# Attention and feed-forward on one core: unsplit float32 products on halves of the array, transposes on VectorE and by SBUF transfers

## The chip, the cores and the metric

The kernel runs on one core of a Trainium2 chip. The time is device time in microseconds (us) of one execution; the number compared is the median of several runs. Five engines work side by side: TensorE (PE, with its weight loads as PEld), VectorE (DVE), ScalarE (ACT), GpSimd (POOL) and SyncE (SP), which here issues all transfers. Matrix products go from SBUF to PSUM; SBUF and PSUM have 128 partitions.

## What is computed

Attention with a threshold, then a feed-forward layer. Inputs are q, k, v of shape (8, 8, 576, 64), a scalar tau, w_in (512, 2048), w_out (2048, 512) and scalars s and b; the output is (4608, 512), all float32.

```python
scores = scale * np.matmul(q, k.transpose(0, 1, 3, 2))       # scale = 1/8
thresh = np.max(scores, axis=-1, keepdims=True) - tau
scores = np.where(scores >= thresh, scores, -1000000000.0)
scores = scores - np.max(scores, axis=-1, keepdims=True)
attn = np.exp(scores)
attn = attn / (np.sum(attn, axis=-1, keepdims=True) + 1e-09)
x = np.matmul(attn, v)              # then (batch, seq, heads * 64)
h = x @ w_in
g = s * np.maximum(h, 0.0) ** 2 + b
out = g @ w_out
```

## The kernel before

Queries are worked on in tiles of 128 rows. A sequence has 576 rows: four full tiles and a tail of 64, and the tails of two heads share one tile. A visit is a batch, a pair of heads and a half of the sequence: four full tiles, and in half of the visits a tail tile. 64 visits make 288 tiles.

For each tile (`tile_of`), scores of 128 queries by 576 keys go to a PSUM bank (L329); VectorE scales and copies them to `sm` with the row's minimum of the negated scores (L332); ScalarE takes exp into `em` (L338); VectorE zeroes what is under the threshold and sums (L341); GpSimd normalizes (L349). TensorE transposes `em` in four blocks of 128 and one of 64 (L358 `tp`, L359 `tt`), because the product with v needs keys on the partitions. The result, 64 columns for each head, goes to `x`.

A float32 number is used in one of two ways. For the first batch (class `Plain`, the first 36 tiles) the products are plain float32, one head at a time: scores with 64 rows of the array, values (L374) with 64 columns. For the others (class `Head`) each operand is split in a high and a low part of type fp32r. The two parts of q lie on the two halves of the rows, those of v on the two halves of the columns, and k and the transposed attention are split in two tensors each; so scores take two products for each half of the keys (L329), and values nine products (L405). The splits cost copies on ScalarE (L279, L287, L292, L389, L391) and subtractions on VectorE (L288, L392, L394, L412) and GpSimd (L280, L293); k, q and part of v are loaded twice, once for each half of the partitions (L250, L258, L263).

The feed-forward layer takes blocks of 256 rows of x: 18 blocks (16 full ones and 2 of tails), with 16 steps for each (`Block.step`). A step makes 12 products of 256 columns into bank `h` (L536), ReLU, square and the high part on ScalarE (L539, L541, L542), the low part on GpSimd (L543), and six products of 512 columns into bank `o` (L549). `Block.stage` splits a block of x (L519, L521). The weights come as float32 and are split once, in 16 groups, on ScalarE and VectorE (`weights`, L466 to L477), into an accurate high and low part.

The order on every engine is written by class `Plan`: each operation is added with an engine, a cost, the keys it reads and writes, and a due time in tiles (`at`). `Plan.run` goes through time with these costs and takes, on each free engine, the ready operation that is due first. Constants set the due times: `LOAD_AHEAD`, `SCORES_AHEAD`, `VALUES_AFTER` and `FFN_AFTER` in tiles, `WEIGHTS_AT` and `WEIGHTS_EACH` for the conversion of weight group f (at `WEIGHTS_AT + WEIGHTS_EACH * f`). `keep_busy` (L677) adds products without use at the start.

Of the kernel before, what the change touches and what calls it, by code (L numbers as in the profile page):

```python
# [22 lines left out]
TWO_BANKS = 16  # L26
WEIGHTS_AT, WEIGHTS_EACH = 12, 1.5
# [80 lines left out]
def tile_attention_ffn(ctx: ExitStack, tc: tile.TileContext, qT, kT, v, tau, w_in, w_out, s, b, out):  # L108


# [14 lines left out]
    HS = S // 2  # L125

# [19 lines left out]
    st = [const(f"st{i}", [P, 8]) for i in range(6)]
    smem = [tuple(const(f"{n}{i}", [P, S + 1]) for n in ("sm", "em")) for i in range(2)]
    qs = [const(f"q{j}", [P, NB], F32R) for j in range(2)]
    raw_head = const("rk", [P, S]), const("rq", [P, S]), const("rv", [P, 5, D])
    xb = [const(f"x{i}", [P, NC, NB]) for i in range(3)]  # L150
    xt = const("xt", [P, NC, 4 * T])
    oo = const("oo", [P, 2, DM])
# [3 lines left out]
        ("s", [P, 2, 512]), ("o", [P, 2, DM]), ("tp", [P, NQ, P]), ("tt", [P, 512]), ("pv", [P, 512]), ("h", [P, 512]))}  # L156
# [4 lines left out]
    def claim(keys, fn):  # L161

        old = [k for k in list(plan.writer) + list(plan.readers) if isinstance(k, tuple) and k[0] == keys[0]]
        plan.add("-", (0, 0), fn, [], list(dict.fromkeys(old)) + keys, -100)


    def split_buffers():
        def e():
            t = sb("e", [P, 9, 3 * P], F32R)
            lazy["ehi"], lazy["elo"] = t[:, 0:5], t[:, 5:9]  # L170

        def k():
            lazy["k"] = sb("k", [P, 4, S], F32R)

        def v_():
            lazy["v"] = sb("v", [P, 3, 5, 2, D], F32R)
        claim(["e"] + [(n, c) for n in ("eh", "el", "et") for c in range(6)], e)
        claim(["k", "khi0", "klo0", "khi1", "klo1"], k)
        claim(["v", "v0", "v1", "v2"], v_)
        claim(["e32", "oo0", "oo1"] + [("x", 2, c, j, u) for c in range(NC) for j in range(2) for u in range(2)], lambda: None)  # L180

    def pe(n, cols, fn, r, w, at):

        plan.add("PE", (n * (0.44 * cols + 6.5), n * (0.44 * cols + 6.5) + 170), fn, r, w, at)
# [4 lines left out]
    def dve2(cost, fn, r, w, at):  # L189
        plan.add("DVE", cost, fn, r, w, at, True)  # L190
# [7 lines left out]
    def dma(kb, fn, r, w, at):  # L198
        plan.add("SP", (max(550, kb * 3.6), 2200 + kb * 3.6), fn, r, w, at)


    class Plain:


        def __init__(self, bi, p_):
            self.bi, self.p, self.tag = bi, p_, ("w%d" % (NF - 1), "v", "k", "e")[p_]
            self.keys = [(self.tag, n) for n in ("k", "q", "v0", "v1")]

        def get(self):
            if self not in lazy:  # L210
                t = sb(self.tag, [P, 2 * S - T + 10 * D], F32)
                lazy[self] = t[:, 0:S], t[:, S:2 * S - T], t[:, 2 * S - T:].rearrange("p (h t d) -> p h t d", h=2, t=5)
            return lazy[self]

        def load(self, at):
            kk, kq = self.keys[:2]
            h2 = slice(2 * self.p, 2 * self.p + 2)
            dma(295, lambda: nc.sync.dma_start(out=self.get()[0], in_=kT[self.bi, h2].rearrange("h d s -> (h d) s")),
                [], [kk], at)
            dma(262, lambda: nc.sync.dma_start(out=self.get()[1], in_=qT[self.bi, h2, :, 0:M].rearrange("h d s -> (h d) s")),  # L220
                [], [kq], at)
            for j in range(2):
                h = 2 * self.p + j
                dma(128, lambda j=j, h=h: nc.sync.dma_start(
                    out=self.get()[2][:, j, 0:NQ], in_=v[self.bi, h, 0:M, :].rearrange("(p t) d -> p t d", t=NQ)),
                    [], [self.keys[2 + j]], at)
                dma(16, lambda j=j, h=h: nc.sync.dma_start(out=self.get()[2][0:T, j, NQ], in_=v[self.bi, h, M:S, :]),
                    [self.keys[2 + j]], [self.keys[2 + j] + (1,)], at)

        def load_tail(self, at):  # L230
            for j in range(2):
                dma(16, lambda j=j: nc.sync.dma_start(
                    out=qd[self.p % 2][j * D:(j + 1) * D, j * T:(j + 1) * T], in_=qT[self.bi, 2 * self.p + j, :, M:S]),
                    [f"qd{self.p % 2}"], [(f"qd{self.p % 2}", j)], at)

    class Head:
        def __init__(self, i, bi, h, q0, q1, tail):
            self.i, self.bi, self.h, self.j, self.q0, self.q1, self.tail = i, bi, h, h % 2, q0, q1, tail

        def load(self, at):  # L240

            q0, q1 = self.q0, self.q1
            rk, rq, rv = raw_head
            self.parts = [], [], []

            def put(which, name, buf, cols, ap, kb):
                for o in 0, D:
                    keys = [(name, o, c) for c in range(cols.start // T, cols.stop // T)]
                    self.parts[which].extend(keys)
                    dma(kb, lambda o=o: nc.sync.dma_start(out=buf[o:o + D, cols], in_=ap), [], keys, at)  # L250

            put(0, "rk", rk, slice(0, S), kT[self.bi, self.h], 144)
            q1_ = S if self.tail and q1 == M else q1
            put(1, "rq", rq, slice(q0, q1_), qT[self.bi, self.h, :, q0:q1_], 64)
            if self.tail and q1_ < S:
                put(1, "rq", rq, slice(M, S), qT[self.bi, self.h, :, M:S], 16)
            self.parts[2].append(("rv", 0))
            dma(128, lambda: nc.sync.dma_start(out=rv[:, 0:NQ, :],  # L258
                                               in_=v[self.bi, self.h, 0:M, :].rearrange("(p t) d -> p t d", t=NQ)),
                [], [("rv", 0)], at)  # L260
            for o in 0, D:
                self.parts[2].append(("rv", 1 + o))
                dma(16, lambda o=o: nc.sync.dma_start(out=rv[o:o + D, NQ, :], in_=v[self.bi, self.h, M:S, :]),  # L263
                    [], [("rv", 1 + o)], at)

        def prepare(self, at):
            pk, pq, pv_ = self.parts
            j = self.j
            rk, rq, rv = raw_head
            q0, m = self.q0, self.q1  # L270
            self.kks, self.kqs, self.kts = [f"khi{j}", f"klo{j}"], [f"q{j}"], [f"qt{j}"]

            def khi():
                return lazy["k"][:, 2 * j]

            def klo():
                return lazy["k"][:, 2 * j + 1]
            self.q, self.ks = (lambda: qs[j]), (lambda: [khi(), klo()])
            act((580, 675), lambda: nc.scalar.copy(out=khi(), in_=rk), pk, [f"khi{j}"], at)  # L279
            pool((1420, 1450), lambda: nc.gpsimd.tensor_tensor(out=klo(), in0=rk, in1=khi().bitcast(F32), op=ALU.subtract),  # L280
                 pk + [f"khi{j}"], [f"klo{j}"], at)

            parts = [(slice(q0, m), qs[j], f"q{j}", (305, 405), (400, 430))]
            if self.tail:
                parts.append((slice(M, S), qt[:, j, j * T:(j + 1) * T], f"qt{j}", (150, 245), (190, 220)))
            for cs, dst, key, ca, cd in parts:
                act(ca, lambda dst=dst, cs=cs: nc.scalar.copy(out=dst, in_=rq[:, cs]), pq, [key], at)  # L287
                dve2(cd, lambda dst=dst, cs=cs: nc.vector.tensor_tensor(  # L288
                    out=dst[D:P], in0=rq[D:P, cs], in1=dst[D:P].bitcast(F32), op=ALU.subtract), pq + [key], [key], at)
            i = self.i % 3  # L290
            self.kvs, self.v = [f"v{i}"], lambda: lazy["v"][:, i]
            act((360, 460), lambda: nc.scalar.copy(out=self.v()[:, :, j, :], in_=rv), pv_, self.kvs, at)  # L292
            pool((850, 885), lambda: nc.gpsimd.tensor_tensor(out=self.v()[:, :, 1 - j, :], in0=rv,  # L293
                                                             in1=self.v()[:, :, j, :].bitcast(F32), op=ALU.subtract),
                 pv_ + self.kvs, self.kvs, at)


    class Group:


        def __init__(self, hd, c0, n, dests):
            self.hd, self.c0, self.n, self.dests, self.blocks = hd, c0, n, dests, []
# [484 lines left out]
```

## Time and profile before

| | |
|---|---|
| runs | 1405.14, 1397.42, 1398.55 us; median 1398.55 |
| profiled execution, first to last instruction | 1402.1 us |
| TensorE busy | 1384.8 us (99%) |
| VectorE busy | 1066.8 us (76%) |
| ScalarE busy | 986.8 us (70%) |
| GpSimd busy | 736.3 us (53%) |
| granted TensorE clock | 1.00 throughout |
| from HBM, to HBM | 88.21 MB, 9.44 MB |

The page gives the profiled execution's span and no time of its own; the span is 3.6 us, or 0.25%, above the median of the runs. Busy time of TensorE is modelled from pipelined records, so the pitch from one start to the next says more than a duration. In a row of the timeline the first number is the start in us from the span's start, the second the length, and xN how many records of one kind are merged; `128*64 128x256` is the part of the array (rows * columns) and the operand's shape. A row of a group shows count, busy us, mean ns of one, and idle time ahead of it with what ended it.

### The profile page before, as it was taken

Reading aid. Unit: us, or ns where it says so; the run is one execution under the profiler, and the core shown is the slowest. Engines: PE = TensorE matmul, PEld = TensorE weight load, DVE = VectorE, ACT = ScalarE, POOL = GpSimd, SP = SyncE. Lnnn points to the kernel's source line nnn. Section 1 sums busy time; section 2 is a strip of 40 time slices with the busy share of each in tenths; the row PEclk is TensorE's granted clock in tenths of the full one; section 3 lists DMA queues with packets and bytes.
Section 4 is the critical chain, followed back from the end, with each engine's and each line's share of the span. In section 5 each row is a group of like instructions: output and inputs, shape, how many; then the busy total and the mean of one; then the engine's idle time right before and its main releaser. Section 6 shows DMA issues by size and latency. Waiting matters only on the chain.

```text
span 1402.1 us, 29393 instructions
## 1 busy us (share of the span) xinstructions
PE 1384.8 (99%) x9369; PEld 1252.3 (89%) x9369; DVE 1066.8 (76%) x3099; ACT 986.8 (70%) x2487; POOL 736.3 (53%) x798
## 2 busy tenths in 40 slices
PE   9999999999999999999999999999999999999998
PEld 7678789889899989998999999999999999999887
DVE  4977568988998898878888787888788887887101
ACT  3777557867777777777777777777777777776443
POOL 1233336656676656655566555665566555564210
PEclk9999999999999999999999999999999999999999
DMA  9701112221222222222122122222222222220000
GB/s 301 248 26 35 29 39 66 82 74 55 79 74 87 63 76 70 81 60 70 52 84 72 55 73 64 83 60 66 65 71 71 70 66 72 64 75 15 16 16 16
DMA packets 94539, 99.59 MB, mean 71 GB/s; under 512 B 34480, under 2 KB 72368, under 8 KB 94384
## 3 DMA queue, kind: packets, MB, share of 16 engines
q1 hardware_dynamic: 94384, 97.71, 23.5%
q8 instruction: 74, 1.21, 0.4%
q14 instruction: 81, 0.66, 0.1%
HBM read 88.21 MB, written 9.44 MB: 70 GB/s over the span
## 4 chain that ended last, share of the span: by engine, by line
PE 93%; DVE 3%; ACT 2%; issue 1%; POOL 0%; DMA 0%; DVEq 0%; SPq 0%; ACTq 0%; POOLq 0%
PE h L536 28%; PE o L549 28%; PE s L329 12%; PE pv L405 9%; PE tp L358 9%; PE pv L374 3%; PE tt L359 2%; DVE em L341 1%; PE h L677 1%; PE h L488 1%; PE o L329 1%; DVE sm L332 1%; DVE e L392 0%; ACT em L338 0%; ACT g L539 0%
## 5 line engine op out<-in xcount | busy, mean ns | idle before, releaser
L536 PE MATMUL h<-xh,w 128*128 128x256 f32 x2304 | 465.5, 285 | 5.0 <-ACT g L539 4.8
L349 POOL TENSOR_SCALAR em<-em,st 128x576 f32<-128x576 f32 x288 | 251.9, 875 | 273.3 <-DVE st L346 113.2
L536 PEld LDWEIGHTS h<-xh,w 128*128 128x128 f32 x2304 | 376.4, 190 | 15.8 <-ACT g L539 8.9
L549 PE MATMUL o<-w,gh 128*128 128x512 f32 x1152 | 369.6, 402 | 0.6 <-ACT g L539 0.5
L543 POOL TENSOR_TENSOR gl<-g,gh 128x256 fp32r<-128x256 f32 x272 | 217.4, 799 | 263.8 <-ACT gh L542 93.6
L536 PE MATMUL h<-xl,w 128*128 128x256 f32 x1152 | 325.4, 282 | 0.2
L341 DVE SCALAR_TENSOR_TENSOR em<-sm,st,em 128x577 f32<-128x577 f32 x288 | 255.3, 887 | 34.5 <-ACT em L338 25.8
L332 DVE TENSOR_SCALAR_CACHE_REDUCE sm<-s 128x576 f32<-128x576 f32 x280 | 211.2, 754 | 89.2 <-PE s L329 86.9
L338 ACT ACTIVATE em<-sm,st 128x576 f32<-128x576 f32 x288 | 224.9, 781 | 49.2 <-DVE sm L332 44.6
L539 ACT ACTIVATE g<-h 128x256 f32<-128x256 f32 x288 | 109.1, 379 | 187.6 <-PE h L536 184.2
L549 PE MATMUL o<-w,gl 128*128 128x512 f32 x576 | 225.9, 392 | 0.1
L536 PEld LDWEIGHTS h<-xl,w 128*128 128x128 f32 x1152 | 219.1, 190 | 5.7 <-DVE xl L521 0.6
L549 PEld LDWEIGHTS o<-w,gh 128*128 128x128 f32 x1152 | 196.4, 189 | 25.9 <-ACT g L539 0.8
L392 DVE TENSOR_TENSOR e<-tp,e 128x512 fp32r<-128x512 f32 (+1 forms) x280 | 178.0, 636 | 53.7 <-ACT e L389 50.0
L389 ACT CAST e<-tp 128x512 fp32r<-128x512 f32 (+1 forms) x280 | 150.5, 538 | 64.3 <-PE tp L358 59.9
L280 POOL TENSOR_TENSOR k<-rk,k 128x576 fp32r<-128x576 f32 x112 | 169.7, 1515 | 45.3 <-ACT k L279 41.9
L358 PE MATMUL tp<-ident,em 128*128 128x128 f32 x1152 | 175.2, 275 | 1.9 <-POOL em L349 0.8
L329 PE MATMUL s<-k,q 128*128 128x288 f32 x896 | 165.4, 306 | 0.3 <-DVE sm L332 0.3
L358 PEld LDWEIGHTS tp<-ident,em 128*128 128x128 f32 x1152 | 137.1, 140 | 26.3 <-issue 5.4
L405 PE MATMUL pv<-e,v 128*128 128x320 f32 (+1 forms) x1008 | 152.6, 296 | 0.0
L405 PEld LDWEIGHTS pv<-e,v 128*128 128x128 f32 x1008 | 141.4, 189 | 2.3
L329 PEld LDWEIGHTS s<-k,q 128*128 128x128 f32 x896 | 130.1, 189 | 4.4 <-DVE sm L332 0.9
(108 smaller groups left out, 1799.3 us busy)
## 6 DMA issues: line engine op xcount, KB each, us to landing
rk<-in_k_dram SPq DMA_DIRECT2D x224, 144.0 KB, 2.8
rv<-in_v_dram SPq DMA_DIRECT2D x112, 128.0 KB, 2.1
rq<-in_q_dram SPq DMA_DIRECT2D x168, 64.0 KB, 2.3
w<-in_moe_w_in_dram SPq DMA_DIRECT2D x16, 512.0 KB, 8.6
w<-in_moe_w_out_dram SPq DMA_DIRECT2D x16, 512.0 KB, 8.7
out_dram<-oo SPq DMA_DIRECT2D x32, 256.0 KB, 2.2
rq<-in_q_dram SPq DMA_DIRECT2D x56, 80.0 KB, 2.4
rv<-in_v_dram SPq DMA_DIRECT2D x224, 16.0 KB, 2.0
```

What stands on the lines that cost most here:

```text
L280: pool((1420, 1450), lambda: nc.gpsimd.tensor_tensor(out=klo(), in0=rk, in1=khi().bitcast(F32), op=ALU.subtract), pk + [f"khi{j}"], [f"klo ...
L329: nc.tensor.matmul(ps[:, hf, 0:HS], stat, kk[:, cs], start=(n == 0), stop=(n == len(seq) - 1))
L332: dve((760, 840), lambda: nc.vector.tensor_scalar(out=get()[0][:, 0:S].rearrange("p (a b) -> p a b", a=2), in0=ps[:, :, 0:HS], scalar1=-SC ...
L338: act((690, 785), lambda: nc.scalar.activation(out=get()[1][:, 0:S], in_=get()[0][:, 0:S], func=AF.Exp, bias=st8[:, 0:1], scale=-1.0), [sm ...
L341: dve2((830, 930), lambda: nc.vector.scalar_tensor_tensor(out=get()[1], in0=get()[0], scalar=st8[:, 1:2], in1=get()[1], op0=ALU.is_le, op1 ...
L349: pool((800, 835), lambda: nc.gpsimd.tensor_scalar(out=get()[1][:, 0:S], in0=get()[1][:, 0:S], scalar1=st8[:, 4:5], scalar2=st8[:, 5:6], o ...
L358: nc.tensor.transpose(out=tp[:, t, :], in_=em[:, t * P:(t + 1) * P], identity=ident)
L392: dve((60 + 560 * big, 140 + 560 * big), lambda hi=hi, lo=lo, cs=cs: nc.vector.tensor_tensor(out=lo(), in0=tp[:, :, cs], in1=hi()[:, 0:NQ] ...
L405: nc.tensor.matmul(ps, g.hd.v()[:, kt, :, :], o[:, kt], start=(n == 0), stop=(n == len(seq) - 1))
L536: nc.tensor.matmul(ps, w[:, c, :], x[:, c, :], start=(i == 0), stop=(i == 3 * NC - 1))
L543: do((715, 750), lambda: eng.tensor_tensor(out=lo, in0=g, in1=hi.bitcast(F32), op=ALU.subtract), [f"g{k}", f"gh{k}"], [f"gl{k}"], at)
L549: nc.tensor.matmul(bank["o"][:, t, :], a[:, ts_], w, start=(f == 0 and i == 0), stop=(f == NF - 1 and i == 2))
```

## The change

No tile is split any more; `Plain`, `Head` and `Group` give way to one class `Visit`. The first batch is treated like the others.

- Scores (`scores`): k and q of a pair of heads are loaded once, one head on partitions 0 to 63 and the other on 64 to 127. One group of four float32 products makes the scores of a tile of both heads, each head on its half of the array's rows, into its own bank (`s0`, `s1`). A tail tile takes two products with all rows.
- Values (`with_v`): one group of ten float32 products for each visit, each head on its half of the array's columns, into one bank.
- Transposes: VectorE transposes blocks of 32 by 32 within `em` into `tr` (two instructions a tile), and four transfers a tile from `tr` to `er`, issued by SyncE, put the blocks where the values' product reads them. The order of keys in v's load follows that.
- Of the small operations, the threshold's addition goes to ScalarE (`AF.Identity`), and the case of an empty row is left to a sum that can't vanish, with the threshold's sign handled once.
- Due times: `VALUES_AFTER` 2 instead of 1, `FFN_AFTER` 2.5 instead of 1.5, weights at 6 + 1.2 f instead of 12 + 1.5 f. `Plan` gets new costs, and VectorE's operations are no longer kept apart from GpSimd's in it. `oo` is one buffer instead of two.

```diff
-LOAD_AHEAD, PREPARE_AHEAD = 6, 2.5
-SCORES_AHEAD, VALUES_AFTER = 1, 1
-FFN_AFTER = 1.5
+LOAD_AHEAD = 6
+SCORES_AHEAD, VALUES_AFTER = 1, 2
+FFN_AFTER = 2.5
-WEIGHTS_AT, WEIGHTS_EACH = 12, 1.5
+WEIGHTS_AT, WEIGHTS_EACH = 6, 1.2
...
+    class Visit:
+        def load(self, at):
+            n, bi, h2 = self.n, self.bi, self.h2
+            dma(295, lambda: nc.sync.dma_start(out=kb[n], in_=kT[bi, h2].rearrange("h d s -> (h d) s")), [], [("k", n)], at)
...
+            for j in range(2):
+                dma(131, lambda j=j: nc.sync.dma_start(
+                    out=vb[n][:, j, 0:NQ], in_=v[bi, 2 * self.pair + j, 0:M, :].rearrange("(c p) d -> p c d", p=P)),
+                    [], [self.kv[j]], at + 1)
...
+    def scores(vs, i, t):
...
+        def pairs():
+            for hf in range(2):
+                cs = slice(hf * HS, (hf + 1) * HS)
+                for j in range(2):
+                    r = slice(j * D, (j + 1) * D)
+                    nc.tensor.matmul(bank[f"s{j}"][:, hf, 0:HS], qb[n][r, t * P:(t + 1) * P], kb[n][r, cs],
+                                     start=True, stop=True)
...
+        def blocks():
+            nc.vector.transpose(out=to[:, :, 0:NQ].rearrange("p m c q -> p m (c q)"),
+                                in_=ev[:, 0:M].rearrange("p (m r) -> p m r", m=4))
+            nc.vector.transpose(out=to[:, 0:2, NQ], in_=ev[:, M:S].rearrange("p (m q) -> p m q", m=2))
+        dve((915, 980), blocks, [em_k], [tr_k], i + 0.5)
+        for n in range(4):
+            jj, e = (n // 2, NB // 32 + n % 2) if t is None else (j, 4 * t + n)
+            plan.add("SP", (450, 2600), lambda n=n, jj=jj, e=e: nc.sync.dma_start(
+                out=er[:, vs.n, jj, e], in_=to[32 * n:32 * n + 32].rearrange("p m c q -> p m (c q)")),
+                [tr_k], [("er", vs.n, jj, e)], i + 0.5)
+
+    def with_v(vs, at):
...
+            for c in range(5):
+                for j in range(2):
+                    nc.tensor.matmul(ps[j * D:(j + 1) * D, 0:32 * nb], vb[n][:, j, c], er[:, n, j, 0:nb, 32 * c:32 * c + 32],
+                                     start=(c == 0), stop=(c == 4))
```

More of the change, by code (lines that the diff above doesn't have):

```diff
@@ L7 @@
 from concourse._compat import with_exitstack
-from concourse.masks import make_identity
 F32 = mybir.dt.float32
@@ L155, in tile_attention_ffn, with pe @@
     bank = {n: pp.tile(sh, F32, name=n) for n, sh in (
-        ("s", [P, 2, 512]), ("o", [P, 2, DM]), ("tp", [P, NQ, P]), ("tt", [P, 512]), ("pv", [P, 512]), ("h", [P, 512]))}
+        ("s0", [P, 2, 512]), ("s1", [P, 2, 512]), ("o", [P, 2, DM]), ("pv", [P, 512]), ("h", [P, 512]))}
     lazy = {}
     plan = Plan()
[L161 to L184, printed above, removed]
+    def pe(cost, fn, r, w, at):
+        plan.add("PE", (cost, cost + 170), fn, r, w, at)
     def dve(cost, fn, r, w, at, port=False):
@@ L189, in dve2 @@
     def dve2(cost, fn, r, w, at):
-        plan.add("DVE", cost, fn, r, w, at, True)
+        plan.add("DVE", cost, fn, r, w, at)
     def act(cost, fn, r, w, at):
@@ L236, in tile_attention_ffn @@
[L236 to L295, printed above, removed]
@@ L328, in scores @@
-                for n, (stat, kk) in enumerate(seq):
-                    nc.tensor.matmul(ps[:, hf, 0:HS], stat, kk[:, cs], start=(n == 0), stop=(n == len(seq) - 1))
-        pe(2 if plain else 4 * len(ti.heads), HS * (3.7 if plain else 1), scores, ti.kq(), [bk], i - SCORES_AHEAD)
-        dve((760, 840), lambda: nc.vector.tensor_scalar(
-            out=get()[0][:, 0:S].rearrange("p (a b) -> p a b", a=2), in0=ps[:, :, 0:HS], scalar1=-SC,
-            scalar2=None, op0=ALU.mult, op1=ALU.min, accum_out=st8[:, 0:1]), [bk], [sm_k, (ks_, 0)], i - SCORES_AHEAD)
@@ L349, in tile_of @@
-        pool((800, 835), lambda: nc.gpsimd.tensor_scalar(
-            out=get()[1][:, 0:S], in0=get()[1][:, 0:S], scalar1=st8[:, 4:5], scalar2=st8[:, 5:6], op0=ALU.mult,
-            op1=ALU.add), [em_k, (ks_, 4), (ks_, 5)], [em_k], i)
-        tp, tt = bank["tp"], bank["tt"][0:T, 0:P]
-        def transposes():
-            em = get()[1]
-            for t in range(NQ):
-                nc.tensor.transpose(out=tp[:, t, :], in_=em[:, t * P:(t + 1) * P], identity=ident)
-            nc.tensor.transpose(out=tt, in_=em[:, M:S], identity=ident)
@@ L654, in tile_attention_ffn @@
-    pairs = [Plain(0, p_) for p_ in range(NP)]
-    heads = [Head(2 * vi + j, vis[0], 2 * vis[1] + j, vis[2] * P, vis[3] * P, vis[4])
-             for vi, vis in enumerate(visits) for j in range(2)]
-    tiles, first = [], {}
-    for vi, vis in enumerate(visits):
-        for ti in make_tiles(vis, *((pairs[vis[1]],) * 2 if vis[0] == 0 else heads[2 * vi:2 * vi + 2])):
-            for hd in ti.heads:
-                first.setdefault(hd, len(tiles))
-            tiles.append(ti)
-    n_plain = sum(ti.plain is not None for ti in tiles)
@@ L666, in tile_attention_ffn, with constants @@
-    pairs[0].load(-30)
+            xs[bi, u] = len(xs) % 3
+            for p_ in range(NP):
+                visits.append(Visit(len(visits), bi, p_, u, (bi > 0 and p_ < NP // 2) == (u == 0)))
+    tiles = []
+    for vs in visits:
+        vs.first = len(tiles)
+        tiles += [(vs, j, t) for t in range(2) for j in range(2)]
+        if vs.tail:
+            tiles.append((vs, 0, None))
+        vs.last = len(tiles) - 1
+    def constants():
+        for t in range(2):
+            nc.gpsimd.memset(sm[t][:, S:S + 1], -3e38)
+            nc.gpsimd.memset(em[t][:, S:S + 1], 1e-9)
+            nc.gpsimd.memset(tr[t][:, 2:4, NQ], 0.0)
+            nc.gpsimd.memset(vb[t][:, :, NQ], 0.0)
+            nc.gpsimd.memset(qd[t], 0.0)
+        nc.gpsimd.memset(zero, 0.0)
@@ L667, in tile_attention_ffn @@
+    pool((900, 900), constants, [], ["sm0", "sm1", "em0", "em1", "tr0", "tr1"] +
+         [("v", n, 2 + m) for n in range(2) for m in range(2)] + [("qd", n, j) for n in range(2) for j in range(2)], -9)
+    visits[0].load(-30)
     dma(0.5, lambda: nc.sync.dma_start(out=tau_t, in_=tau.partition_broadcast(P)), [], ["tau"], -20)
@@ L692, in tile_attention_ffn @@
     events = []
-    for p_, pr in enumerate(pairs):
-        if p_:
-            events.append((0, lambda pr=pr: pr.load(first[pr] - LOAD_AHEAD)))
-        t = n_plain - 5 * (NP - p_) + 2
-        events.append((0 if p_ < 2 else t - 9, lambda pr=pr, t=t: pr.load_tail(t - 6)))
-    events.append((n_plain - 0.2, split_buffers))
-    for hd in heads:
-        if hd in first:
-            events.append((n_plain - 0.1 if first[hd] < n_plain + 1 else first[hd] - 0.5,
-                           lambda hd=hd: (hd.load(first[hd] - LOAD_AHEAD), hd.prepare(first[hd] - PREPARE_AHEAD))))
+    for n, vs in enumerate(visits):
+        events.append((vs.first - 0.5 if n else -1, lambda vs=vs, n=n: n and vs.load(vs.first - LOAD_AHEAD)))
     converted = set()
@@ new lines, in tile_attention_ffn, with block @@
+            events.append((i, lambda j=j: keep_busy(BUSY_EACH, [f"s{j}"])))
+        if i != vs.last:
+            continue
+        events.append((i + 0.1, lambda vs=vs, i=i: with_v(vs, i + VALUES_AFTER)))
+        blocks = []
+        if vs.pair == NP - 1:
+            blocks.append(("full", vs.bi, vs.u))
+            if vs.u and vs.bi % 4 == 3:
+                blocks.insert(0 if vs.bi == B - 1 else 1, ("tail", vs.bi // 4, 0))
+        for k_ in blocks:
+            when = max(when, i + FFN_AFTER)
+            each = 1.2 if i < 100 else 1.0
+            def block(k_=k_, when=when, step=step, i=i, each=each):
+                blk = make_block(*k_)
+                blk.stage(max(i + FFN_AFTER, when - 1))
+                for f in range(NF):
+                    convert(f)
+                    blk.step(f, when + each * f)
+                    if not step and f % 4 == 3:
+                        sums(f // 4, when + each * f)
+                blk.finish(when + each * (NF + 1))
+            events.append((i + 0.2, block))
+            when += each * NF
+            step += NF
```

308 lines of the change are left out of this document (84 added, 224 removed).

## The prediction

> **What bounds the kernel now.** I read the page's engine table first, then the chain that ended last, then rows of the timeline on TensorE.
>
> ```profile
> span 1402.1 us, 29393 instructions
> ...
> PE 1384.8 (99%) x9369; PEld 1252.3 (89%) x9369; DVE 1066.8 (76%) x3099; ACT 986.8 (70%) x2487; POOL 736.3 (53%) x798
> ...
> q1 hardware_dynamic: 94384, 97.71, 23.5%
> ...
> PE 93%; DVE 3%; ACT 2%; issue 1%; POOL 0%; DMA 0%; DVEq 0%; SPq 0%; ACTq 0%; POOLq 0%
> PE h L536 28%; PE o L549 28%; PE s L329 12%; PE pv L405 9%; PE tp L358 9%; PE pv L374 3%; PE tt L359 2%; DVE em L341 1%; PE h L677 1%; PE h L488 1%; PE o L329 1%; DVE sm L332 1%; DVE e L392 0%; ACT em L338 0%; ACT g L539 0%
> ```
>
> TensorE is busy 99% of the span and carries 93% of the chain; it idles 1402.1 - 1384.8 = 17 us. So what counts is how many columns TensorE streams. The feed-forward part (L536, L549) is 56% of the chain and isn't edited; attention is 36%, of which the transposes (tp, tt) are 11%, some 150 us. Two more rows date the first feed-forward product, about 80 us, and price one step of it (12 products of 256 columns, 6 of 512):
>
> ```profile
> L536 PE MATMUL h<-xh,w x24: 278/283/386, 79.8 to 88.7; 128*128 128x256 f32 x24
> ...
> 702.31 1.43 PE h L536 x12
> 704.29 1.39 PE o L549 x6
> ```
>
> A step is 2.82 us; 288 steps are 812 us, with L488 (0.5% of the span) 819. From 79.7 to 1402 there are 1322 us. Less 819, less 5 at the end behind the last product, less 11 of idle time, leaves 487 us for attention behind the start.
>
> **TensorE's new attention.** The transposes go, 150 us. Scores and values change from single passes on split halves to unsplit float32. The first batch already runs such products (64*128 scores, 128*64 values), so its rows price them. Starts count, since durations overlap:
>
> ```profile
> 42.82 0.40 PE L329 MATMUL s<-k 64*128 64x288 f32 x1
> 43.55 0.40 PE L329 MATMUL o<-k 64*128 64x288 f32 x1
> 44.74 0.38 PE L374 MATMUL pv<-x,v 128*64 128x128 f32 x2
> 45.18 0.27 PE L374 MATMUL pv<-x,v 128*64 128x128 f32 x1
> ...
> 82.73 0.75 PE L329 MATMUL s<-w 64*128 64x288 f32 x2
> 83.08 0.65 PE L329 MATMUL s<-w 64*128 64x288 f32 x2
> 83.57 0.40 PE L329 MATMUL s<-w 64*128 64x288 f32 x1
> 83.90 0.39 PE L536 MATMUL h<-xh,w 128*128 128x256 f32 x1
> 84.12 0.28 PE L536 MATMUL h<-xl,w 128*128 128x256 f32 x1
> 84.24 0.28 PE L536 MATMUL h<-xh,w 128*128 128x256 f32 x1
> ...
> 109.36 0.28 PE L536 MATMUL h<-xh,w 128*128 128x256 f32 x1
> 109.56 0.32 PE L374 MATMUL pv<-oo,v 128*64 128x128 f32 x1
> 109.72 0.38 PE L374 MATMUL pv<-oo,v 128*64 128x128 f32 x2
> ```
>
> Each product leaves two records, called passes here. Three passes of 288 columns lie between the first two rows, 0.243 us each; four of 128 between the next two, 0.110 each. On that line 256 columns cost 0.216 and 320 cost 0.270. The other rows price a change of array shape: the last score pass takes 0.33 instead of 0.243 when a 128*128 product follows (0.09 lost), and the first pass in the new shape 0.22 instead of 0.12 (0.10). Entering 64*128 loses 0.10 on its first pass (82.73 to 83.08), entering 128*64 loses 0.08 to 0.09 and then 0.05.
>
> The program's order shows the places. On TensorE in mid-kernel, before (s scores, pv values, tp and tt transposes, h and o feed-forward):
>
> ```order
> L536 MATMUL h<-xh_7463,w_1379 128x256
> L329 MATMUL s<-k,qt 128x288 x8
> L405 MATMUL pv<-e,v 128x320 x9
> L549 MATMUL o<-w_1269,gh_96 128x512 x2
> L549 MATMUL o<-w_1269,gl_98 128x512
> L549 MATMUL o<-w_1269,gh_96 128x512 x2
> L549 MATMUL o<-w_1269,gl_98 128x512
> L358 MATMUL tp<-ident,em_82 128x128 x4
> L359 MATMUL tt<-ident,em_82 64x128
> ```
>
> And on TensorE mid-kernel now, scores of two heads between two feed-forward products (s_104 and s_105 are the heads' banks):
>
> ```order
> L385 MATMUL h<-xh_4191,w_722 128x256
> L211 MATMUL s_104<-k_85,q_87 128x288
> L211 MATMUL s_105<-k_85,q_87 128x288
> L211 MATMUL s_104<-k_85,q_87 128x288
> L211 MATMUL s_105<-k_85,q_87 128x288
> L385 MATMUL h<-xh_4191,w_807 128x256
> ```
>
> Transposes have left the queue, and each score group now stands alone between 128*128 products. In the whole new order the shape changes 361 times, 17 of them before the first feed-forward product.
>
> Whether the two halves of the array work side by side no row of before shows: no two products on different halves stand next to each other there. The bounds are full overlap and none. I take overlap, with starts and ends in program order: passes A1 A2 B1 B2 of two products then fill 3 slots, a score group of four products 5 slots instead of 8, a value group of ten products 11 instead of 20. Behind the first feed-forward product stand 117 score groups, 31 pairs of tail products and 60 value groups (28 of 256 columns, 32 of 320):
>
> - scores 117 x 5 x 0.243 = 142
> - tails, full array, 31 x 4 x 0.243 = 30
> - values 28 x 11 x 0.216 + 32 x 11 x 0.270 = 162
> - shape changes 344 x 0.09, and 0.10 (0.05 for the 62 into 128*64) = 62
>
> Sum 396 us instead of 487: TensorE saves 91. Without overlap it would be 396 + 85 (scores) + 132 (values) = 613.
>
> The Trainium skill, TensorE: Matmul & The Clock Gate, section Part 3: Packing small matmuls, gives packed products a span of one product plus about 4 ns for each further tile; by that rule groups need 4 and 10 slots and the sum falls by some 43. Its table measures 2.38 times for three column tiles, 79% of ideal; by that the value groups take 12.6 slots and the sum rises by about 23. No row here shows either.
>
> **The start.** VectorE loses the splits (L392, L394, L288, L412) and gains two transposes a tile. What moved is the weight conversion. On VectorE ahead of the first staging of x, before (L521 is the staging, L469, L471 and L477 the conversion):
>
> ```order
> L471 SCALAR_TENSOR_TENSOR xl_544<-w_404,xl_544 128x512
> L469 TENSOR_SCALAR xh_615<-xh_615 128x512
> L341 SCALAR_TENSOR_TENSOR em_82,st_78<-sm_81,st_78,em_82 128x577
> L332 TENSOR_SCALAR sm_79,st_73<-s 128x576
> L344 RECIPROCAL st_78<-st_78 128x1
> L346 TENSOR_SCALAR st_78<-st_78 128x1
> L335 TENSOR_SCALAR st_73<-st_73,tau_t 128x1
> L521 TENSOR_TENSOR xl_684<-x_88,xh_683 128x512 x2
> ```
>
> And now on VectorE (L370 the staging; L318, L320, L326 the conversion):
>
> ```order
> L318 TENSOR_SCALAR xl_685<-xl_685 128x512
> L320 SCALAR_TENSOR_TENSOR xl_685<-w_661,xl_685 128x512
> L238 STREAM_TRANSPOSE tr_83<-em_81 128x4x128
> L240 STREAM_TRANSPOSE tr_83<-em_81 128x2x32
> L326 TENSOR_TENSOR w_722<-xl_685,w_722 128x512 x2
> L230 SCALAR_TENSOR_TENSOR em_81,st_73<-sm_79,st_73,em_81 128x577
> L318 TENSOR_SCALAR xh_732<-xh_732 128x512
> L233 RECIPROCAL st_73<-st_73 128x1
> L238 STREAM_TRANSPOSE tr_82<-em_80 128x4x128
> L240 STREAM_TRANSPOSE tr_82<-em_80 128x2x32
> L370 TENSOR_TENSOR xl_737<-x_93,xh_736 128x512 x2
> ```
>
> Ahead of the staging stood 13, 12 and 10 conversion steps; now 29, 28 and 28. Starts in this stretch price them:
>
> ```profile
> L332 DVE TENSOR_SCALAR_CACHE_REDUCE sm<-s 128x576 f32<-128x576 f32 x280 | 211.2, 754 | 89.2 <-PE s L329 86.9
> ...
> 6.76 0.76 DVE L332 TENSOR_SCALAR_CACHE_REDUCE sm<-s 128x576 f32<-128x576 f32 x1 [6.76 <-PE s L329]
> ...
> 63.01 0.69 DVE L471 SCALAR_TENSOR_TENSOR xh<-w,xh 128x512 int32<-128x512 int32 x1
> 63.62 0.16 DVE L344 RECIPROCAL st<-st 128x1 f32<-128x1 f32 x1
> ...
> 65.31 0.20 DVE L335 TENSOR_SCALAR st<-st,tau_t 128x1 f32<-128x1 f32 x1
> 65.43 0.41 DVE L469 TENSOR_SCALAR xl<-xl 128x512 int32<-128x512 int32 x1
> 65.76 0.81 DVE L341 SCALAR_TENSOR_TENSOR em<-sm,st,em 128x577 f32<-128x577 f32 x1
> 66.50 0.08 DVE L341 DVE_READ_ACCUMULATOR em<-sm,st,em 128x1 f32 x1
> 66.50 0.68 DVE L477 TENSOR_TENSOR w<-xh,w 128x512 fp32r<-128x512 f32 x1
> 67.10 0.15 DVE L344 RECIPROCAL st<-st 128x1 f32<-128x1 f32 x1
> 67.18 0.13 DVE L346 TENSOR_SCALAR st<-st 128x1 f32<-128x1 f32 x1
> 67.23 0.74 DVE L332 TENSOR_SCALAR_CACHE_REDUCE sm<-s 128x576 f32<-128x576 f32 x1
> 67.90 0.08 DVE L332 DVE_READ_ACCUMULATOR sm<-s 128x1 f32 x1
> ```
>
> Start to start: L469 0.33, L471 0.61, L477 0.60, L341 0.74, L344 0.08, L332 0.67, L335 0.12, L346 0.05. A transpose of 512 columns lies between L469 and L477 (0.33 to 0.60); I take 0.60, the dearer of two rows that both write 512 words a partition, and 0.13 for the small one (as L335): 0.73 a tile. The new order needs 21 x 0.67 + 20 x 0.82 + 19 x 0.73 = 44 for tiles and 44 for conversion. The old one needed about 31 + 18 = 48, in the 73 us from 6.8 to 79.7, so a third of its time went in waits. The row of L332 puts nearly all of its idle time, over the whole run, down to score products; those come sooner now, two tiles to a group, so I put 9 us of waits: first feed-forward product at 6.8 + 88 + 9 + 1 = 105, between 95 (cheap transposes, no waits) and 122 (the old waits). That loses 25.
>
> **What stays hidden.** VectorE in all: 288 x 2.22 = 640 us, conversion 49, the rest some 45: 734 of 1231 behind the start. ScalarE drops its split copies and gains one 128x1 operation a tile; GpSimd drops two of four jobs. Both were under TensorE and get lighter. SyncE gets 1152 transfers that turn blocks of 32 into rows, waits on VectorE for each four, and loads of later visits queue behind them: 1675 issues in the order instead of 944.
>
> ```profile
> 31.05 2.31 SPq L434 DMA_DIRECT2D w<-in_moe_w_out_dram  x1
> ...
> 76.48 2.52 SPq L250 DMA_DIRECT2D rq<-in_q_dram  x4
> ```
>
> An unhindered issue is 0.63 us, 1055 in all, hidden in 1336 with a fifth to spare. Packets grow to about 256 thousand; at the old mean (23.5% of 16 engines over 94384, 56 ns) that is 67% of the engines. Values stand two tiles behind their last tile, some 9 us, against a few us of issue and landing.
>
> **Sum.** 105 + 819 + 396 + 11 idle + 5 = 1336 us of span. The profiled span is 0.25% above the median of the runs, 1398.55; so 1333.
>
> **Rivals.** *No overlap on the array halves*, which ends on the other side: each pass waits for the one ahead. It gives 1336 + 217 = 1553, scores alone 1421, values alone 1468. The gain is 66 of 217, so below 70% of the overlap the kernel is slower. For it speaks that nothing in the trace shows overlap; against it that 128*64 and 64*128 products are set apart by a shape change, so the array is at least set in halves. The Trainium skill (same page and section) lets a weight load pass a running product only on other rows, which would hit the column halves; the rows at 44.74 and 45.18, all on the same rows, keep a pitch of 0.110 without such a gap. I give both failing 0.07, one alone 0.09.
>
> *SyncE becomes the bound*: with issues like the one at 31.05 (2.31 us, behind queued weights) among them, a mean of 0.84 us makes 1402. Only the start has such queues now; 0.9 would give 1508. Chance 0.07, ending at 1380 to 1510.
>
> *A late start*, waits as before and TensorE idle meanwhile: 1355 to 1385. Chance 0.12. *Tighter packing* (4 and 10 slots) gives 1290. Chance 0.10, the forecast itself 0.55.
>
> A change within 0.5%, 1391.6 to 1405.5, can't be told from none. Faster: 0.55 + 0.12 + 0.10 + part of SyncE's, 0.79; slower 0.18. The range 1285 to 1425 takes in tight packing, the late start and scores without overlap.
>
> **What would show it.** Right: score groups with a pitch near 1.4 us including entry, values near 2.4 and 3.0, the first feed-forward product near 105 us, PE under 95% busy, tp and tt gone. Wrong: score groups of 1.9 us or more; TensorE waiting on transfers of er; SyncE without gaps between issues.

## The result and the profile after

The changed kernel takes 1329.52 us (median, 1329.04 to 1331.58), the kernel before 1401.65 us in the same comparison (1397.42 to 1405.14): a ratio of 0.9484, 95% interval 0.9450 to 0.9519. The profiled execution has a span of 1329.8 us. These are the rows of its page that were shown of the kernel before, with the row of the granted clock (PEclk: tenths of the full TensorE clock, in 40 equal slices of the span). In the chain, a q behind an engine's name (SPq) is its queue, where it waits or issues transfers:

```profile
span 1329.8 us, 24065 instructions
...
PE 1250.4 (94%) x7689; PEld 970.6 (73%) x7689; DVE 832.7 (63%) x2205; ACT 680.9 (51%) x1639; POOL 503.0 (38%) x577
...
PEclk7559999999999999999999999999999999999999
...
q1 hardware_dynamic: 283696, 167.88, 47.9%
...
PE 78%; DVE 7%; DMA 6%; SPq 4%; issue 2%; ACT 2%; POOL 0%; DVEq 0%; ACTq 0%; POOLq 0%
PE o L398 28%; PE h L385 27%; PE pv L255 12%; PE s L211 9%; DMA er<-tr 5%; SPq L244 3%; PE s L202 2%; DVE sm L221 1%; DVE em L230 1%; DVE tr L238 1%; ACT em L227 1%; DMA w<-in_moe_w_in_dram 1%; DVE w L326 1%; DMA out_dram<-oo 1%; SPq L192 0%
```

The transposes tp and tt (11% of the chain) are gone. TensorE idles 1329.8 - 1250.4 = 79 us instead of 17, 48 of them in the first 106 us, where the granted clock is also low (third row). Rows of TensorE's timeline date the first feed-forward product (105.89 us) and show one score group and one value group with the products next to them. The two rows at 710.63 are windows of a few ns, one after the other; the second holds one record more:

```profile
105.89 0.38 PE L385 MATMUL h<-xh,w 128*128 128x256 f32 x1 [0.99 <-ACT xh L368]
...
710.63 0.51 PE L211 MATMUL s<-k,q 64*128 64x288 f32 x1
710.63 0.51 PE L211 MATMUL s<-k,q 64*128 64x288 f32 x2
710.98 0.65 PE L211 MATMUL s<-k,q 64*128 64x288 f32 x4
711.22 0.65 PE L211 MATMUL s<-k,q 64*128 64x288 f32 x4
711.80 0.73 PE L398 MATMUL o<-w,gh 128*128 128x512 f32 x2
...
769.87 0.39 PE L398 MATMUL o<-w,gl 128*128 128x512 f32 x1
770.19 2.91 PE L255 MATMUL pv<-er,v 128*64 128x320 f32 x20
773.03 0.73 PE L398 MATMUL o<-w,gh 128*128 128x512 f32 x2
```

The second record adds nothing to the length: the passes of a pair, one of each head, start 7 ns apart in the records. Eight passes of 288 columns take four slots, 710.63 to 711.80, and 1.17 us is 4 x 0.243 + 0.10 for entering + 0.09 for leaving. All 117 groups behind the first feed-forward product have a median of 1.171. A value group of 20 passes takes 2.84 us: ten slots of 0.27 and the change of shape.

### The profile page after: what moved, and what is told of

The parts are those of the page before. It is cut to its first block, busy times and chain, and to the rows that moved or that the text cites. A ratio compares the mean times of both kernels' runs of the same rounds, so it can differ in the third digit from the quotient of the medians.

```text
span 1329.8 us, 24065 instructions
## 1 busy us (share of the span) xinstructions
PE 1250.4 (94%) x7689; PEld 970.6 (73%) x7689; DVE 832.7 (63%) x2205; ACT 680.9 (51%) x1639; POOL 503.0 (38%) x577
## 2 busy tenths in 40 slices
DMA packets 283822, 169.41 MB, mean 127 GB/s; under 512 B 105008, under 2 KB 268848, under 8 KB 283696
## 3 DMA queue, kind: packets, MB, share of 16 engines
q1 hardware_dynamic: 283696, 167.88, 47.9%
## 4 chain that ended last, share of the span: by engine, by line
PE 78%; DVE 7%; DMA 6%; SPq 4%; issue 2%; ACT 2%; POOL 0%; DVEq 0%; ACTq 0%; POOLq 0%
PE o L398 28%; PE h L385 27%; PE pv L255 12%; PE s L211 9%; DMA er<-tr 5%; SPq L244 3%; PE s L202 2%; DVE sm L221 1%; DVE em L230 1%; DVE tr L238 1%; ACT em L227 1%; DMA w<-in_moe_w_in_dram 1%; DVE w L326 1%; DMA out_dram<-oo 1%; SPq L192 0%
## 5 line engine op out<-in xcount | busy, mean ns | idle before, releaser
L234 POOL TENSOR_SCALAR em<-em,st,zero 128x576 f32<-128x576 f32 x288 | 283.6, 986 | 459.0 <-DVE st L233 308.6
L221 DVE TENSOR_SCALAR_CACHE_REDUCE sm<-s,nsc 128x576 f32<-128x576 f32 x288 | 227.5, 809 | 123.2 <-PE s L211 83.2
L238 DVE STREAM_TRANSPOSE tr<-em 128x512 f32<-128x512 f32 x288 | 204.1, 709 | 156.6 <-DMA er<-tr 93.6
L211 PE MATMUL s<-k,q 64*128 64x288 f32 x1024 | 175.5, 446 | 33.3 <-DVE sm L221 24.3
L255 PE MATMUL pv<-er,v 128*64 128x256 f32 (+1 forms) x1280 | 188.0, 424 | 14.7 <-DMA er<-tr 12.4
L255 PEld LDWEIGHTS pv<-er,v 128*64 128x64 f32 x1280 | 99.0, 141 | 93.4 <-issue 41.2
L211 PEld LDWEIGHTS s<-k,q 64*128 64x128 f32 x1024 | 96.3, 193 | 81.2 <-DVE sm L221 32.2
L398 PEld LDWEIGHTS o<-w,gl 128*128 128x128 f32 x576 | 108.2, 188 | 28.4 <-POOL gl L392 3.1
L391 ACT CAST gh<-g 128x256 fp32r<-128x256 f32 x288 | 115.9, 402 | 15.1 <-PE o L398 8.9
L390 ACT ACTIVATE g<-g 128x256 f32<-128x256 f32 x288 | 119.2, 414 | 6.6
```

The costliest lines, as they stand in the source:

```text
L211: nc.tensor.matmul(bank[f"s{j}"][:, hf, 0:HS], qb[n][r, t * P:(t + 1) * P], kb[n][r, cs], start=True, stop=True)
L221: dve((745, 830), lambda: nc.vector.tensor_scalar(out=sb_[:, 0:S].rearrange("p (a b) -> p a b", a=2), in0=ps[:, :, 0:HS], scalar1=nsc, sca ...
L234: pool((900, 940), lambda: nc.gpsimd.tensor_scalar(out=ev, in0=ev, scalar1=st8[:, 4:5], scalar2=zero, op0=ALU.mult, op1=ALU.add), [em_k, ( ...
L238: nc.vector.transpose(out=to[:, :, 0:NQ].rearrange("p m c q -> p m (c q)"), in_=ev[:, 0:M].rearrange("p (m r) -> p m r", m=4))
L255: nc.tensor.matmul(ps[j * D:(j + 1) * D, 0:32 * nb], vb[n][:, j, c], er[:, n, j, 0:nb, 32 * c:32 * c + 32], start=(c == 0), stop=(c == 4))
L390: act((290, 390), lambda: nc.scalar.activation(out=g, in_=g, func=AF.Square), [f"g{k}"], [f"g{k}"], at)
```

## Experiments

All edits are made to the changed kernel; its own time to compare with is 1329.5 us, ratio 0.9484.

### Do the halves overlap, and does that hang on the order of the products?

score_order issues both products of one head, then both of the other:

```diff
-            for hf in range(2):
+            for j in range(2):
...
-                for j in range(2):
+                for hf in range(2):
```

> The changed kernel, with the four score products of a group in another order: both products of the first head, then both of the second. Theory A (each half of the array has its own queue, so the second head need not wait for the first): as the changed kernel, 1330 us, and a group's first products of both heads still start within 0.01 us. Theory B (products start in program order, and overlap only because neighbours lie on different halves): 7 slots of 0.243 us instead of 4, 128 x 3 x 0.243 = 93 us more, some 1415.

Measured: 1330.53 us, 0.9479 (0.9451 to 0.9506), and 117 groups with a median of 1.177 us; the passes of a pair start 13 ns apart instead of 7. For the time, the order of four products does not matter.

value_order does the same to the ten products of the values:

```diff
-            for c in range(5):
-                for j in range(2):
+            for j in range(2):
+                for c in range(5):
```

> The changed kernel, with the ten value products of a visit in another order: five of the first head, then five of the second. Theory A (own queues, looking ahead over ten products): as the changed kernel, 1330 us. Theory A with a short look-ahead: in between. Theory B (program order): 19 slots instead of 10.5, 8.5 x (32 x 0.216 + 32 x 0.270) = 132 us more, some 1460.

Measured: 1393.61 us, 0.9929 (0.9903 to 0.9956), in between. TensorE's timeline shows one group between its neighbours, in windows of a few ns. Such a window holds two records where passes come one by one (each still runs when the next begins), and four where they come in pairs:

```profile
818.42 0.28 PE L385 MATMUL h<-xh,w 128*128 128x256 f32 x1
818.63 0.48 PE L255 MATMUL pv<-er,v 128*64 128x320 f32 x1
...
819.75 0.70 PE L255 MATMUL pv<-er,v 128*64 128x320 f32 x2
...
820.29 0.76 PE L255 MATMUL pv<-er,v 128*64 128x320 f32 x4
...
822.50 0.70 PE L255 MATMUL pv<-er,v 128*64 128x320 f32 x2
...
823.13 0.39 PE L385 MATMUL h<-xh,w 128*128 128x256 f32 x1
```

Six passes start one by one from 818.63 to 820.02, 0.27 apart; from 820.29 to 821.10 four pairs; then six single ones to 822.77. That is 6 + 4 + 6 = 16 slots instead of 10. The records do not name the head, but ten passes of each head, each in its own order, fill 16 slots in this way only if the second head starts when the first has four of its passes, two products, left. So TensorE does not need the products in strict alternation, but it looks only a few of them ahead. Six more slots in 60 groups are 6 x (28 x 0.216 + 32 x 0.270) = 88 us; idle time behind the first feed-forward product falls from 25 to 9 us, which leaves 72. Some value groups of the changed kernel last longer than the median, so by the records the groups take 83 us more, not 88; that leaves 66 or so, and 64 are measured.

scores_full_rows takes the overlap from the scores: q is padded with zeros to all 128 rows, one slot for each head.

```diff
-                    r = slice(j * D, (j + 1) * D)
-                    nc.tensor.matmul(bank[f"s{j}"][:, hf, 0:HS], qb[n][r, t * P:(t + 1) * P], kb[n][r, cs],
+                    nc.tensor.matmul(bank[f"s{j}"][:, hf, 0:HS], qb[t][:, j], kb[n][:, cs],
```

> The changed kernel, with q of each head padded with zeros to 128 rows, so that scores use the whole array one head after the other: no overlap and no change of shape for scores. q comes in four transfers a visit instead of one. If the overlap is worth 4 slots (0.97 us a group) and the shape changes cost 0.38 us a group: 0.59 x 117 = 69 us more, 1399. If the shape change were free, 0.97 x 117 = 114 more, 1444. If TensorE weren't the bound: 1330.

Measured: 1425.93 us, 1.0156 (1.0122 to 1.0191), 1.6% above the kernel before and 27 us above the expected 1399. Its first feed-forward product and one score group, then TensorE's waits for q in this run and in the changed kernel (a row of waits gives us in all, how many, and the longest):

```profile
118.92 0.39 PE L387 MATMUL h<-xh,w 128*128 128x256 f32 x1 [0.99 <-ACT xh L370]
...
748.38 2.10 PE L213 MATMUL s<-k,q 128*128 128x288 f32 x8
```

```profile
PE s L213 <- DMA q<-in_q_dram: 20.4, 4, 10.7
```

```profile
PE s L211 <- DMA q<-in_q_dram: 8.8, 2, 4.6
```

Eight passes now take eight slots (their starts lie 0.242 apart), and no change of shape comes with them: 117 x (4 x 0.243 - 0.19 - 0.19) = 69 us. (A group loses 0.19 to entering its shape and leaving it, and the products on both sides lose another 0.19. By the records, score and feed-forward passes take 70 us more.) Of the other 25 of the 94 us between the spans, 13 are a later first product, most of it because the four smaller loads of q come late there (20.4 us of waits instead of 8.8), 7 are idle time behind it, and 5 are longer value groups. So the overlap of the scores, less its shape changes, is worth some 70 us by itself; without it, and with these smaller costs, the gain of the change is gone.

### Is TensorE the bound?

extra_products puts five products without use (128 columns, all rows) ahead of each score group:

```diff
+            for _ in range(5):
+                nc.tensor.matmul(bank["s0"][:, 0, 0:P], ones.bitcast(F32), ones.bitcast(F32), start=True, stop=True)
```

> The changed kernel, with five float32 products of 128 columns without use ahead of each score group, in its bank: ten passes of 0.110 us, as many as the transposes of two tiles took before. Theory: TensorE's stream is the bound, and the gain came from taking the transposes off it. 117 groups behind the start x 1.1 = 129 us more, less what falls in TensorE's 25 us of waits: 1435 to 1460. Rival (the gain came from elsewhere and TensorE has slack): under 1360.

Measured: 1435.04 us, 1.0227 (1.0199 to 1.0254), 105.5 us more. The added passes are 117 x 10 x 0.110 = 129 us behind the first feed-forward product; idle time there fell from 25 to 8 us. That gives 112. Value groups take 7 us less in all than in the changed kernel, which leaves 105; 103 us lie between the spans and 105.5 between the medians. TensorE is the bound, with some 17 us of slack that added work can fill.

### How near is SyncE?

more_issues cuts two of a tile's four er transfers in two, 576 issues more for the same bytes:

```diff
+                for a, b in ((0, 96), (96, 160)) if n < 2 else ((0, 160),):
+                    nc.sync.dma_start(out=er[:, vs.n, jj, e, a:b], in_=src[:, :, a:b])
```

> The changed kernel, with two of the four transfers of each tile into er cut in two (96 and 64 words a row): the same bytes, 576 more issues on SyncE. SyncE was busy with issues for 1005 us in the changed kernel, about 0.646 us from one issue of er to the next. Theory (SyncE is next to bind): 1005 + 73 between issues + 372 = 1450 us of SyncE, so the time is 1455 to 1490. Rival (issues have slack, or short ones are cheaper): 1330 to 1350.

Measured: 1633.17 us, 1.1663 (1.1625 to 1.1701): SyncE binds, and harder than expected. First the row of the transfers' line in the changed kernel (shortest, median and longest issue in ns, then the first and last start in us), with VectorE's waits for it, then the same of this run, then three rows of this run's TensorE waits and its clock in mid-run (busy us and records of PE, PEld, DVE, ACT, POOL, then granted clock, share of the DMA engines, GB/s):

```profile
L244 SPq DMA_DIRECT2D er<-tr x1152: 542/602/2020, 13.1 to 1216.8; - x192
...
  DVE tr L238: 93.6, 70
```

```profile
L247 SPq DMA_DIRECT2D er<-tr x1728: 542/594/1947, 13.0 to 1523.7; - x192
...
  DVE tr L238: 419.2, 183
```

```profile
PE pv L257 <- DMA er<-tr: 101.2, 58, 5.3
PE h L387 <- ACT g L390: 53.4, 33, 7.2
PE o L400 <- DVE oo L411: 30.6, 10, 4.8
```

```profile
400.00:800.00 400.00, 337.21 (x1894) 248.12 (x1893) 206.72 (x562) 161.23 (x399) 129.59 (x147) 0.91 0.41 102
```

The last er transfer is issued at 1523.7 us, and 112 us of feed-forward work stand behind it; in the changed kernel it is 1216.8, with 113 us behind. Up to that point SyncE issued 2243 transfers here, one each 0.661 us, and stood still for 42 us: 2243 x 0.661 + 42 = 1524. The expected 1455 to 1490 us are about what the issues alone take; what comes behind the last of them was left out. By the same count the changed kernel issues 1667 at 0.657 us, 1095 of 1217 us: a tenth to spare. The bytes are the same and the DMA engines less busy (0.41 in the window above), so it is the issues and not the data. The low clock of that window, 0.91, comes with the waits. Behind stops TensorE can run at half its clock for some microseconds; here two stops of 1.3 us lie within 4 us:

```profile
827.19 0.72 PE L257 MATMUL pv<-er,v 128*64 128x320 f32 x2 [1.33 <-DMA er<-tr]
829.17 3.15 PE L257 MATMUL pv<-er,v 128*64 128x320 f32 x12 [1.26 <-DMA er<-tr]
```

```profile
829.10:832.00 2.90, 2.83 (x12) 1.35 (x14) 2.54 (x7) 0.96 (x2) 0.94 (x1) 0.52 0.48 139
```

Twelve passes take 3.15 us, where the 20 at 770.19 took 2.91 in the changed kernel: the granted clock is 0.52 from 829.1 to 832. Not every stop does this. Of the five stops of 1.5 to 1.8 us that the changed kernel has behind its first feed-forward product, four leave the clock at 1.00.

### What sets the start?

In the changed kernel VectorE is busy nearly without a break up to the first feed-forward product (columns as above):

```profile
20.00:40.00 20.00, 11.20 (x41) 5.27 (x38) 18.67 (x46) 11.10 (x22) 6.06 (x5) 0.59 0.86 245
40.00:60.00 20.00, 10.04 (x30) 4.86 (x30) 19.41 (x46) 11.84 (x22) 3.65 (x4) 0.59 0.83 263
60.00:80.00 20.00, 11.56 (x38) 7.07 (x40) 19.76 (x48) 11.32 (x23) 4.10 (x4) 0.59 0.89 278
80.00:106.00 26.00, 10.02 (x39) 5.04 (x35) 24.57 (x57) 15.19 (x28) 3.30 (x4) 0.54 0.86 264
```

VectorE stands at 82.4 of 86 us, but the DMA engines at 0.83 to 0.89 too. Two runs hold back the conversion of weight groups, from group 4 or from group 8 on, until the first block of x is done:

```diff
-                [kr], [kt] if u else [tag, kt, (tag, 1)], at)
+                [kr] + ([("x", 0, NP - 1)] if f >= 4 else []), [kt] if u else [tag, kt, (tag, 1)], at)
```

> The changed kernel, with the conversion of weight groups 4 to 15 held back until the first block of x is there: ahead of the first staging VectorE has 12, 11 and 8 conversion steps instead of 29, 28 and 28. Theory (VectorE's work sets the start): 17 x 0.33 + 17 x 0.61 + 20 x 0.60 = 28 us less, first feed-forward product at 78 us, time 1302; the later groups need 3.1 us each on VectorE beside 2.2 for a tile, more than TensorE's 4.4 us for a step and a tile, which gives some 12 us back: 1302 to 1315. Rival (the transfers set the start): 1325 to 1335.

> The same with groups 8 to 15 held back: 20, 19 and 16 steps ahead of the staging, 16 us less on VectorE. Theory (VectorE sets the start): first feed-forward product at 90 us and 1312 to 1318, nothing given back. Rival (the transfers set the start): 1325 to 1335.

Measured: 1355.13 us, 0.9677 (0.9649 to 0.9704), and 1338.56 us, 0.9555 (0.9525 to 0.9585); both slower than the changed kernel and outside both expected ranges. The first product comes at 106.1 and 105.5 us, as before. The windows and VectorE's waits of the first of the two show why:

```profile
60.00:80.00 20.00, 8.80 (x36) 4.61 (x36) 7.57 (x21) 3.48 (x7) 2.46 (x3) 0.57 0.89 292
80.00:106.00 26.00, 8.23 (x32) 4.34 (x32) 12.21 (x33) 7.08 (x14) 3.29 (x4) 0.59 0.89 272
```

```profile
DVE tr L238 <- DMA er<-tr: 20.9, 7, 5.6
DVE em L230 <- ACT em L227: 9.1, 10, 1.5
```

VectorE is relieved of 29 us (65 busy of 106 instead of 94), and waits for er transfers instead: they free the tr buffers, and share the DMA engines with 29 weight loads of 512 KB (28 in the same window of the changed kernel). Behind the first product the held conversion is missed: idle time of TensorE there is 42 and 30 us instead of 25. So two more runs hold the conversion of groups 8 to 15 and their loads as well, the loads until the first block of x is done (loads_late_8) or only until its third pair's values are (loads_late_8b). Shown is w_in in loads_late_8; w_out is held alike:

```diff
-            [], wkeys(f), at)
+            [("x", 0, NP - 1)] if f >= 8 else [], wkeys(f), at)
```

> Conversion of weight groups 8 to 15 held until the first block of x is complete, and their loads (16 of 512 KB, 8.4 MB) held as well. Holding the conversion alone left the first feed-forward product where it was (105.5 against 105.9 us), while VectorE then waited 20.9 us for er transfers (4 groups held back further), with the DMA engines 86% busy from 20 to 106 us. Theory (two bounds one behind the other, VectorE's work and the transfers that share the DMA engines with weight loads): 8.4 of 22.6 MB and 24 us of VectorE leave the stretch, so the first feed-forward product comes at 82 to 93 us; the loads then have to arrive during the first 8 steps, which costs 8 to 20 us of waits; time 1312 to 1335. Rival (the latency of the steps of a tile, one after the other, sets the start): the first product stays within 3 us of 106, time 1335 to 1360.

> As the run before, but the loads of groups 8 to 15 wait only for the third pair of heads' values of the first block (some 20 us earlier), the conversion for the fourth. Two bounds: the loads fall into the last quarter of the start, so part of the gain is lost there: first feed-forward product at 92 to 102 us, few waits behind it; time 1312 to 1328. Latency of a tile's steps: first product at 103 to 109 us and 1330 to 1342.

Measured: 1340.26 us, 0.9559 (0.9523 to 0.9595), and 1343.72 us, 0.9579 (0.9546 to 0.9612). In loads_late_8 the first product comes 11 us earlier:

```profile
95.01 0.38 PE L385 MATMUL h<-xh,w 128*128 128x256 f32 x1
```

It is the only one of the four in which it does, and it differs from convert_late_8 in the loads alone, so transfers are part of what sets the start; the expected 82 to 93 us were not reached, so two bounds do not explain it all. The 11 us are lost again behind it, where idle time grows from 25 to 37 us. The passes behind it take some 7 us more as well, in part at a lower clock (0.99 instead of 1.00 from 106 to 400 us), so the run ends later than the changed kernel. In loads_late_8b, just above its slower expected range, the held loads fill the end of the start (DMA share 0.96 from 80 to 106 us), VectorE waits 12.5 us at once for a tr buffer, and the first product comes at 107.7 us. What sets the start below 95 us stays open.

### A version that beats both

TensorE's three longest waits in the changed kernel, over the whole span:

```profile
PE s L211 <- DVE sm L221: 24.3, 12, 8.8
PE pv L255 <- DMA er<-tr: 12.4, 11, 2.7
PE h L385 <- ACT g L388: 10.0, 13, 1.8
```

values_later lets the values stand three tiles behind their last tile instead of two, and the feed-forward steps a tile later too:

```diff
-SCORES_AHEAD, VALUES_AFTER = 1, 2
-FFN_AFTER = 2.5
+SCORES_AHEAD, VALUES_AFTER = 1, 3
+FFN_AFTER = 3.5
```

> VALUES_AFTER 3 instead of 2 and FFN_AFTER 3.5 instead of 2.5. TensorE waits 12.4 us for er transfers at the values' products, 5 of them behind the start. If values a tile later suffice: these 5 us go, less the later end of the last visit (up to 4): 1324 to 1331. Rival: the first block of x comes a tile later, some 4 us, with nothing gained elsewhere: 1331 to 1338.

Measured: 1320.51 us, 0.9416 (0.9385 to 0.9447), 9 us less than the changed kernel and under the expected 1324 to 1331. The first product comes at 105.6 us, as there; idle time of TensorE behind it is 16 us instead of 25. Two of its waits, over the whole span:

```profile
PE pv L255 <- DMA er<-tr: 8.4, 4, 3.3
PE h L385 <- ACT g L388: 6.8, 15, 0.5
```

Most of the er waits in this run lie in the start. Behind the first feed-forward product they fall from 5.1 to 0.4 us, those for ScalarE (g) from 10.0 to 6.8, and those for `oo` from 4.0 to 2.4. So the transfers are about half of the 9 us.

Two more runs ask which constant it was, and whether 4 and 4.5 are better still:

> FFN_AFTER 3.5 alone, VALUES_AFTER stays 2. If the 9 us came from values that no longer wait for er transfers: this one stays at 1327 to 1333. If they came from the feed-forward steps that start later behind their block: 1318 to 1324.

> VALUES_AFTER 4 and FFN_AFTER 4.5 (2 and 2.5 in the changed kernel, 3 and 3.5 in the run before, which was 9 us faster with 9 us less idle time of TensorE behind the first feed-forward product, 16.3 against 25.3). If the lag of the values was still short: a few of the 16 us go, 1312 to 1320. If a lag of 3 already covers issue and landing, and more only delays the first block of x and the last visit: 1320 to 1328.

Measured: with FFN_AFTER 3.5 alone 1331.22 us, 0.9504 (0.9463 to 0.9546), no gain; with 4 and 4.5 1322.61 us, 0.9437 (0.9403 to 0.9472), no more than with 3 and 3.5. With the feed-forward lag at 3.5 in both, a third tile of lag for the values takes 1331 to 1321 us: it is the lag of the values that pays, and three tiles are enough. VALUES_AFTER 3 with FFN_AFTER left at 2.5 was not run.

## Why the prediction was right

The forecast was 1333 us (a span of 1336); 1329.5 (1329.8) came. The mechanism holds: TensorE is the bound, and the halves of its array work side by side. That the total is off by only 4 us is partly luck, since two errors, of 24 and 14 us, go against each other. Term by term, from 0 to the end of the span (1322.5 is the start of the last product):

| term | forecast, us | measured, us |
|---|---|---|
| first feed-forward product | 105 | 105.9 |
| feed-forward steps | 819 | 819 (taken as forecast) |
| attention behind it | 396 | 372 (1322.5 - 105.9 - 819 - 25.3) |
| idle behind it | 11 | 25.3 |
| end | 5 | 7.3 |

- **Overlap** is the step that carried the sign, and it holds: score groups of 1.17 us and value groups of 2.84, with about 70 us for the scores alone shown by scores_full_rows. The rivals without overlap, of both or of one, fall; value groups show no loss on the column halves beyond their ten slots.
- **The slots** were wrong: starts in program order would have made 5 and 11, and there are 4 and 10, since the first passes of both heads start together. So the case that was given 0.55 had the packing wrong, and the one that was given 0.10 had it right. The rule of the Trainium skill (TensorE: Matmul & The Clock Gate, Part 3: Packing small matmuls) is a span of one product and about 4 ns for each further tile. These groups come close to it, with 7 ns between the two starts. The rival of tighter packing gave 1290, 43 us less than the forecast; of these 24 came. Value groups explain 7 of the missing 19: they last 3.01 and 2.42 us on the mean here, 2.87 and 2.33 in extra_products, where they hardly wait. The other 12 are small pieces that were not assigned.
- **Idle time** was sized too low, 11 against 25 us. The largest part, 10.0 us, is feed-forward products that wait for ScalarE (g); the er transfers have 5.1, since values two tiles behind did not always cover issue and landing; products that wait for VectorE to write `oo`, now a single buffer, have 4.0. In values_later 9 us of this go, and the time falls by as much. This error and the slots' cancel in good part.
- **Shape changes** cost what the rows of before had said: 0.10 on the first pass (711.80 to the next, 0.338 instead of 0.23) and 0.09 on the last.
- **The end** was taken from before, 5 us. With one buffer `oo`, VectorE's last two results start 2.9 us apart instead of 0.7, so it took 7.3.
- **The start** came out in its sum, less in its terms. VectorE is busy 94 of 106 us, where the forecast had 88 of work; its waits between its first scores and the first feed-forward product are 4 us and not 9 (two transposes a tile take 0.75 to 0.76 us against 0.73). That VectorE alone sets the start was wrong: with 29 us less of its work the first product did not come earlier. Transfers beside the weight loads stand right behind.
- **SyncE** is a near miss: "a fifth to spare" set 1055 us against the whole span. An issue measured 0.65 to 0.66 us, but the issues have to be done 113 us before the end, so a tenth is spare. (The count before the change is 947, not 944, and 60 groups enter 128*64 behind the start, not 62; neither changes the sum.) The DMA engines were far less loaded than the 67% forecast, 47.9%: 283696 packets at 36 ns instead of 56.

For the rivals this means that, by this count, SyncE would have bound with some 10% more for each issue, not 33%. Its chance was too low, and so was that of tighter packing.

## What to carry to other kernels

When work moves from the binding engine to an issue queue, count the issues against the time in which they must be done, not against the span; add some for a test, as here, and see where the time turns. Unsplit float32 on halves of the array is worth its two passes where two independent products stand next to each other in the queue: keep them within a few products of each other, and let the work that waits for transfers stand one more step behind. A stretch in which an engine and the DMA engines are both near full may not get shorter when the engine alone is relieved: here 29 us less of VectorE's work gained nothing.

## What was not expected of the hardware

- Two products on different halves of the rows, or of the columns, start their passes 7 ns apart, although each makes two passes; the second one does not wait for the second pass of the first.
- A product further down in the queue passes one ahead of it on the other half: in value_order the second head begins when the first has four passes left, and so ahead of the first head's last product. The Trainium skill (TensorE: Matmul & The Clock Gate, Part 3: Packing small matmuls) says that products start and end in program order. The 16 slots here do not agree with that: in program order the second head could run beside the last product of the first at most, which makes 18.
- Two stops of TensorE of 1.3 us within 4 us come with a granted clock of 0.52 for 2.9 us (more_issues), while four of five single stops of 1.5 to 1.8 us in the changed kernel leave it at 1.00. At the start of the changed kernel, with TensorE half idle, it is 0.54 to 0.59 from 20 to 106 us.
